# Maxima and sums of eight query blocks in one tile, transposed by one matmul: a kernel of windowed attention mixed with a Fourier layer

## The chip, the cores and the metric

The kernel runs on one core of one Trainium2 chip. The core has five engines that work side by side, each through its own queue in order: TensorE (PE, matrix products; PEld is its weight load), VectorE (DVE), ScalarE (ACT), GpSimd (POOL) and SyncE (SP), which here does nothing but issue DMAs. The metric is the device time of one execution in microseconds (us), lower is better.

## The reference

The input is x of 2048 rows and 512 columns. A gate mixes two layers of it:

```
g = sigmoid((x * gate_w).sum(-1))
a = Cr @ (x @ Wr.T) - Ci @ (x @ Wi.T)      # Fourier layer: 512 wide inside, 2048 x 2048 outside
q, k, v = split(x @ wqkv)                  # 32 heads of 16
p = softmax(q k^T / 4, where 0 <= i - j < 256)
b = (p v) @ wo
out = g * a + (1 - g) * b
```

All values are float32. The inputs make large scores, so the softmax needs its row maxima.

## The kernel before, in words

Dense products (projections, Fourier layer, output) keep float32 precision by a split: every operand is a high part, rounded to the fast matmul type, and a low part, and each product is three fast matmuls (TERMS, line 217).

Attention goes over N = 4 x 32 = 128 steps n: four head groups g of eight heads, 32 blocks of 64 queries. A tile holds four head pairs p (NP = 4), two heads above each other in its 128 rows. Each step does two things, LAG = 20 steps apart.

First, `s_pair(n, p)` (line 314): PE computes the scores of 64 queries of two heads against up to 320 keys (line 324); DVE adds the mask and takes the row minimum of the negated score into a column of `nm` (line 326, one custom instruction and a read of its accumulator, both recorded at that line); ACT takes the exponential and its row sum into a column of `l` (line 329). The scores themselves are then dropped. A group u of eight steps fills 32 columns of `nm` and 32 of `l`: one for each pair and step.

Second, 20 steps later, `t_pair(k, p)` (line 386) computes the transposed scores with the maximum already subtracted, because the maxima stand as extra rows (96 to 99) of `ring[0]`: PE (line 393), exponential by ACT (line 394), masking by POOL (lines 399 and 403). `pv` (line 406) multiplies with the values (line 420) into a PSUM tile `o`; every eighth block the result is multiplied with the reciprocal sums `rl` (line 430), which come from DRAM.

Between the two, the maxima and sums have to turn from columns into rows. That is what the change touches. After group u is complete, in the loop of line 680 at pair p = 2 of a step, behind `pv`:

- `m_rows(u)`: a matmul of `nm` with the identity transposes it into a PSUM tile (line 336); DVE writes minus it as high and low part (lines 339, 340); SP stores that to `m_scr[u]` in DRAM (line 341).
- `l_rows(u)`: DVE takes the reciprocal of `l` (line 350); a second matmul transposes it into another PSUM tile (line 352); DVE copies it to `lt` (line 354); SP stores it to `l_scr[u]` in two pieces (line 357).
- `m_ring(u)`, one step later: ACT's queue loads `m_scr[u]` into rows 96 to 99 of `ring[0]` (line 346).

These two matmuls have full float32 operands, which PE runs as two passes each; a pass has its own weight load.

All DMAs through `ld` (line 55) are issued by SP in order and are recorded at line 56. So one queue holds the stores above, the loads of the ring (`ring<-qk_scr`), of values (`vr<-v_scr`), of Fourier matrices (`raw<-cr`, `raw<-ci`) and of the Fourier layer's inner results (`big<-ab_scr`).

PSUM tiles of scores, transposes and output blocks come from one pool of four buffers (`ps_a`, tag "st"): whoever takes a buffer waits until the last reader of what it held before is done.

What sets the order: on PE it is the program's (line 673). Between the attention's matmuls, `fill` (line 665) takes a fixed number of dense matmuls from the generator `dense`, so PE's queue always holds some. On DVE, ACT, POOL and SP a scheduler, which simulates the kernel while it is built, chooses the order. `make_pad` (line 298) builds, from the ring, the block-diagonal query tiles (`pad`) that the scores of the following steps use as weights. `load_split` and `split_raw` (lines 97 to 105) load a piece of a Fourier matrix into `raw` and split it, by casts at line 80 and subtractions at line 81.

Of the kernel before, what the change touches and what calls it, by code (L numbers as in the profile page):

```python
# [7 lines left out]
F32 = mybir.dt.float32  # L8
# [6 lines left out]
P = 128  # L15
# [4 lines left out]
NP = 4  # L20
# [12 lines left out]
def fnet_window_mix(ctx: ExitStack, tc: tile.TileContext, xT, x, wqk, wv, wr, wi, cr, ci, wo, gw, out):  # L33
    nc = tc.nc
# [3 lines left out]
    st = ctx.enter_context(tc.tile_pool(name="st", bufs=3))  # L38
    ev = ctx.enter_context(tc.tile_pool(name="ev", bufs=5))
    at = ctx.enter_context(tc.tile_pool(name="at", bufs=2))  # L40
    ps_a = ctx.enter_context(tc.tile_pool(name="ps_a", bufs=4, space=PSUM))
# [9 lines left out]
    l_scr = [dram.tile([NP, 2, 512], F32, name=f"l_scr{i}") for i in range(16)]  # L51
# [3 lines left out]
    def ld(dst, src):  # L55
        mark("sp", nc.sync.dma_start(dst, src))

    def f(ap):
        return ap.bitcast(F32)
# [4 lines left out]
    def mark(e, ins):  # L64
        last[e] = ins.ins

    @contextmanager
    def behind(*engines):
        with ExitStack() as es:
            for e in engines:  # L70
                if e in last:
                    es.enter_context(tc.issue_after(last[e]))
            yield
# [51 lines left out]
    with tc.manual_schedule(engines={mybir.EngineType.Activation, mybir.EngineType.DVE, mybir.EngineType.SP}):  # L125
# [12 lines left out]
        for dk in range(DK):  # L138
            c = slice(dk * 256, dk * 256 + 256)
# [17 lines left out]
    ident = const.tile([P, P], F32, name="ident")  # L157
# [6 lines left out]
    for t, edges in ((half, ((0, 16, 32, 48, 64, 80), (16, 32, 48, 64, 80, 96))), (mrow, ((96, 98), (98, 100)))):  # L164
        nc.gpsimd.memset(t, 0.0)
        for h in range(2):
            for i, e in enumerate(edges[h]):
                a = t[:, h:h + 1]
# [3 lines left out]
    def clear_rows(i, ss):  # L172
        nc.gpsimd.memset(f(ring[i][96:128, :, ss * 512:(ss + 1) * 512]), 0.0)
# [7 lines left out]
    def clear_pads():  # L181
        for t in vpad:
            nc.gpsimd.memset(t, 0.0)
        for t in pads[1]:
            nc.gpsimd.memset(f(t[96:128]), 1.0)
            for h in range(2):
                a = t[96:128, :, 64 * h:64 * h + 64]
                nc.vector.tensor_scalar(a, f(a), mrow[96:128, h:h + 1], None, op0=OP.mult)
# [109 lines left out]
    def make_pad(i, n):  # L298
        if not 0 <= n < NG * NB:
            return  # L300
        t = pads[i][n % NPAD]
        b = n % NB
        with behind(*(("act", "dve") if n < NPAD else ())):
            for h in range(2):
                src, dst = f(ring[i][:96, :, b * BQ:(b + 1) * BQ]), t[:96, :, 64 * h:64 * h + 64]
                if i and h:
                    nc.scalar.activation(dst, src, AF.Copy, scale=half[:96, h:h + 1])  # L307
                else:
                    nc.vector.tensor_scalar(dst, src, half[:96, h:h + 1], None, op0=OP.mult)  # L309
        PAD[i, n] = t  # L310

    ML = {}

    def s_pair(n, p):
        j = n % NB
        u, jj = divmod(n, 8)
        if jj == 0 and p == 0:
            ML[u] = [at.tile([P, NP * 8], F32, name="nm"), at.tile([P, NP * 8], F32, name="l")]
        nm, l = ML[u]
        k0 = max(0, (j - 4) * BQ)  # L320
        w = (j + 1) * BQ - k0
        c = slice(p * 8 + jj, p * 8 + jj + 1)
        ps = ps_a.tile([P, 512], F32, name="s", tag="st")
        nc.tensor.matmul(ps[:, :w], PAD[0, n][:, p], ring[1][:, p, k0:k0 + w], start=True, stop=True)  # L324
        sm = at.tile([P, WIN], F32, name="sm", bufs=3)
        mark("dve", nc.vector.tensor_tensor_reduce(out=sm[:, :w], in0=ps[:, :w], in1=mask[:, WIN - w:],  # L326
                                                   scale=1.0, scalar=3e38, op0=OP.add, op1=OP.min,
                                                   accum_out=nm[:, c]))
        mark("act", nc.scalar.activation(sm[:, :w], sm[:, :w], AF.Exp, bias=nm[:, c], scale=-1.0,  # L329
                                         accum_out=l[:, c]))  # L330

    def m_rows(u):
        U = u % 4
        nm = ML[u][0]
        pt = ps_a.tile([P, 512], F32, name="s", tag="st")
        nc.tensor.matmul(pt[:32, :P], nm, ident, start=True, stop=True)
        hl = at.tile([32, 2, 2, 64], F32R, name="mhl", bufs=1)
        m = pt[:32, :P].rearrange("c (a r) -> c a r", a=2)
        nc.vector.tensor_scalar(hl[:, :, 0], m, -1.0, None, op0=OP.mult)
        nc.vector.scalar_tensor_tensor(hl[:, :, 1], m, -1.0, f(hl[:, :, 0]), op0=OP.mult, op1=OP.subtract)  # L340
        ld(m_scr[u].rearrange("x p (j r) -> (p j) x r", r=64), f(hl[:]).rearrange("c a h r -> c (a h) r"))

    def m_ring(u):
        U = u % 4
        with behind("act"):
            nc.scalar.dma_start(f(ring[0][96:100, :, U * 512:(U + 1) * 512]), m_scr[u])

    def l_rows(u):
        l = ML.pop(u)[1]
        nc.vector.reciprocal(l, l)  # L350
        pt = ps_a.tile([P, 512], F32, name="s", tag="st")
        nc.tensor.matmul(pt[:32, :P], l, ident, start=True, stop=True)
        lt = at.tile([32, P], F32, name="lt", bufs=1)
        nc.vector.tensor_copy(lt, pt[:32, :P])
        for a in range(2):
            ls = l_scr[u]
            ld(bass.AP(tensor=ls.tensor, offset=ls.offset + a * 512, ap=[[1024, NP], [64, 8], [1, 64]]),
               lt[:, 64 * a:64 * a + 64])

    OT = {}  # L360
    V2 = {}
# [4 lines left out]
    def v_load(n):  # L366
        if n >= NG * NB:
            return
        g, kb = divmod(n, NB)
        raw = at.tile([P, 4, 64], F32, name="vr", bufs=1)  # L370
        for h in range(2):
            ld(raw[64 * h:64 * h + 64].rearrange("r (c j) x -> r c j x", j=2),
               v_scr[kb // 4][:, :, h, g, :].rearrange("c (j r) x -> r c j x", r=64))
        VR[n] = raw

    def v_spread(n):
        if n >= NG * NB:
            return
        raw = VR.pop(n)
        v2 = vpad[n // 4 % 2]  # L380
        for h in range(2):
            r = slice(64 * h, 64 * h + 64)
            nc.gpsimd.tensor_copy(v2[r, :, :, 16 * h:16 * h + 16], raw[r].rearrange("r j (p d) -> r j p d", d=16))  # L383
        V2[n // 4] = v2
# [262 lines left out]
    def need(key):  # L647
        while key not in have:
            next(stream)
# [3 lines left out]
    def ring_ahead(n):  # L653
        nonlocal loaded
        while loaded < 16:
            g, ss = divmod(loaded, 4)
            if n >= 32 * g + 8 * ss:
                need(("qk", g, ss))
            if ("qk", g, ss) not in have or n - LAG < 32 * (g - 1) + 8 * ss + 9:
                break  # L660
            with behind(*(("sp",) if g == 0 else ())):
                ring_load(g, ss)
            loaded += 1

    def fill(n):
        nonlocal quota
        rate = FILL_FIRST if n < LAG else FILL_SEQ if "proj" in have else FILL_PROJ
        quota += rate / 2
        while quota >= 1:
            next(stream, None)  # L670
            quota -= 1
# [3 lines left out]
    maxima = sent = 0  # L675
# [4 lines left out]
    for n in range(N + LAG + 2):  # L680
        if n in (1, 3, 5):
            for i in range(2):
                clear_rows(1 - i, (n + 1) // 2)
        if n == 7:
            clear_pads()
        k = n - LAG
        ring_ahead(n + 1)
        if -4 <= k < N - 4 and k % 4 == 0:
            for c in range(2):
                need(("v", (k + 4) % NB // 2 + c))  # L690
            with behind(*(("sp",) if k < 4 else ())):
                v_load(k + 4)
        if -4 <= k and k % 4 == 3:
            v_spread(k + 1)
        if n == 0:
            make_pad(0, 0)
        for p in range(NP):
            if n < N:
                s_pair(n, p)
            fill(n)  # L700
            if 0 <= k < N:
                t_pair(k, p)
            if p == 0:
                make_pad(0, n + 1)
                if k >= -1:
                    make_pad(1, k + 1)
            fill(n)
            if p == 2 and sent < maxima:
                m_ring(sent)
                sent += 1  # L710
            if p == 2 and k % 3 == 0:
                for j in range(k - 3, k):
                    if 0 <= j < N:
                        pv(j)
                if maxima < 16 and n > 8 * maxima + 8:
                    m_rows(maxima)
                    l_rows(maxima)
                    maxima += 1
    attention_done()
    for _ in stream:  # L720
# [45 lines left out]
```

## Time and profile before

| | us |
|---|---|
| median of 3 runs | 873.67 |
| lowest and highest | 871.34, 877.32 |
| profiled execution: its own time | 873.98 |
| profiled execution: span of the profile | 872.2 |
| mean granted TensorE clock | 0.998 |

The page of the profile gives the costliest groups of instructions. A line there reads: source line, engine, operation, output and inputs by the program's names, shapes, count, then busy time in us and mean ns of one, then the engine's idle time just before them and what ended it.

```profile
L451 PE MATMUL dc<-big,hi 128*128 128x512 f32 x1024 | 356.0, 396 | 0.0
L329 ACT ACTIVATE sm<-sm,nm 128x320 f32<-128x320 f32 (+4 forms) x512 | 277.9, 544 | 49.4 <-DVE nm L326 47.9
L326 DVE CUSTOM_DVE_ANT_0 sm<-s,mask 128x320 f32<-128x320 f32 (+4 forms) x512 | 231.7, 461 | 95.8 <-PE s L324 75.3
L324 PE MATMUL s<-ring,pad 128*128 128x320 f32 (+4 forms) x512 | 158.4, 309 | 4.3 <-DVE nm L326 3.9
```

Matmuls overlap, so the mean of one is more than what it adds to the queue. The answers about the lines of the change, in ns (minimum, median, maximum), are:

```profile
L336 PE MATMUL s<-ident,nm x32: 272/273/297, 73.2 to 681.0; 128*32 128x128 f32 x32
L352 PE MATMUL s<-ident,l x32: 272/273/273, 73.4 to 681.2; 128*32 128x128 f32 x32
L339 DVE TENSOR_SCALAR mhl<-s x16: 274/279/279, 73.6 to 681.3; 32x128 fp32r<-32x128 f32 x16
L354 DVE COPY lt<-s x16: 268/278/280, 73.8 to 681.5; 32x128 f32<-32x128 f32 x16
L350 DVE RECIPROCAL l<-l x16: 336/343/353, 64.2 to 664.2; 128x32 f32<-128x32 f32 x16
```

Sixteen groups, two passes each, make 32 records for a matmul. Attention with its groups lies between 34 and 753 us of the span; the rest is the start and the end of the dense work.

### The profile page before, as it was taken

Reading aid. Unit: us, or ns where it says so; the run is one execution under the profiler, and the core shown is the slowest. Engines: PE = TensorE matmul, PEld = TensorE weight load, DVE = VectorE, ACT = ScalarE, POOL = GpSimd, SP = SyncE. Lnnn points to the kernel's source line nnn. Section 1 sums busy time; section 2 is a strip of 40 time slices with the busy share of each in tenths; the row PEclk is TensorE's granted clock in tenths of the full one; section 3 lists DMA queues with packets and bytes.
Section 4 is the critical chain, followed back from the end, with each engine's and each line's share of the span. In section 5 each row is a group of like instructions: output and inputs, shape, how many; then the busy total and the mean of one; then the engine's idle time right before and its main releaser. Section 6 shows DMA issues by size and latency. Waiting matters only on the chain.

```text
span 872.2 us, 17214 instructions
## 1 busy us (share of the span) xinstructions
PE 860.1 (99%) x5192; PEld 693.5 (80%) x5192; DVE 601.9 (69%) x1966; ACT 581.4 (67%) x1793; POOL 387.8 (44%) x1067
## 2 busy tenths in 40 slices
PE   9999999999999999999999999999899999999998
PEld 7888778787878778788787887878678787788886
DVE  4588986667879987778787777878585444564431
ACT  5488799888988888788788877878676454111110
POOL 9100154445536746656465666554466665200000
PEclk9999999999999999999999999999999999999999
DMA  7865686465758537634355353589644332376541
GB/s 244 286 218 172 217 253 191 161 207 174 235 171 262 173 95 222 173 116 154 121 148 151 121 143 122 149 282 293 209 144 139 117 119 103 127 265 191 190 145 49
DMA packets 90829, 153.70 MB, mean 176 GB/s; under 512 B 26864, under 2 KB 35824, under 8 KB 90736
## 3 DMA queue, kind: packets, MB, share of 16 engines
q1 hardware_dynamic: 89984, 151.42, 55.3%
q10 hardware_dynamic: 752, 1.18, 0.4%
q8 instruction: 41, 0.67, 0.3%
q14 instruction: 52, 0.43, 0.2%
HBM read 104.60 MB, written 47.97 MB: 175 GB/s over the span
## 4 chain that ended last, share of the span: by engine, by line
PE 91%; DMA 5%; DVE 2%; ACT 1%; issue 0%; SPq 0%; DVEq 0%; ACTq 0%
PE dc L451 39%; PE dab L265 9%; PE s L324 8%; PE o L420 8%; PE dqk L243 8%; PE t L393 8%; PE dv L265 5%; PE t L638 5%; DMA qk_scr<-hl 2%; DMA ring<-qk_scr 1%; DMA big<-ab_scr 1%; DVE sm L326 1%; DMA pt<-wqk 1%; PE s L231 0%; DVE pad L309 0%
## 5 line engine op out<-in xcount | busy, mean ns | idle before, releaser
L451 PE MATMUL dc<-big,hi 128*128 128x512 f32 x1024 | 356.0, 396 | 0.0
L399 POOL TENSOR_SCALAR_AFFINE_SELECT pt<-pt 64x128 f32<-64x128 f32 x512 | 192.7, 376 | 274.0 <-ACT pt L394 257.7
L329 ACT ACTIVATE sm<-sm,nm 128x320 f32<-128x320 f32 (+4 forms) x512 | 277.9, 544 | 49.4 <-DVE nm L326 47.9
L326 DVE CUSTOM_DVE_ANT_0 sm<-s,mask 128x320 f32<-128x320 f32 (+4 forms) x512 | 231.7, 461 | 95.8 <-PE s L324 75.3
L394 ACT ACTIVATE pt<-t 128x320 f32<-128x320 f32 (+4 forms) x512 | 209.0, 412 | 93.0 <-PE t L393 91.1
L451 PEld LDWEIGHTS dc<-big,hi 128*128 128x128 f32 x1024 | 186.6, 188 | 32.8 <-issue 2.5
L451 PE MATMUL dc<-big,lo 128*128 128x512 f32 x512 | 201.8, 394 | 0.0
L403 POOL TENSOR_SCALAR_AFFINE_SELECT pt<-pt 64x128 f32<-64x128 f32 x448 | 165.6, 370 | 0.0
L324 PE MATMUL s<-ring,pad 128*128 128x320 f32 (+4 forms) x512 | 158.4, 309 | 4.3 <-DVE nm L326 3.9
L393 PE MATMUL t<-ring,pad 128*128 128x320 f32 (+4 forms) x512 | 154.7, 302 | 0.3 <-DVE nm L326 0.3
L309 DVE TENSOR_SCALAR pad<-ring,half 96x256 fp32r<-96x256 f32 x384 | 120.4, 356 | 28.0 <-PE t L393 22.5
L324 PEld LDWEIGHTS s<-ring,pad 128*128 128x128 f32 x512 | 96.1, 188 | 38.6 <-issue 8.5
L393 PEld LDWEIGHTS t<-ring,pad 128*128 128x128 f32 x512 | 96.3, 188 | 18.7 <-DVE nm L326 1.4
L451 PEld LDWEIGHTS dc<-big,lo 128*128 128x128 f32 x512 | 96.4, 188 | 10.8
L81 DVE TENSOR_TENSOR lo<-raw,hi 128x512 fp32r<-128x512 f32 x146 | 98.9, 708 | 1.3 <-PE dc L451 1.3
L329 ACT ACTIVATION_READ_ACCUMULATOR sm<-sm,nm 128x1 f32 x512 | 99.1, 194 | 0.0
L265 PE MATMUL dab<-hi,big 128*128 128x512 f32 x256 | 91.1, 396 | 0.9 <-DVE hl L88 0.9
L243 PE MATMUL dqk<-big,hi 128*128 128x512 f32 x240 | 86.6, 394 | 1.1 <-DVE hl L86 0.5
L80 DVE CAST hi<-raw 128x512 fp32r<-128x512 f32 x142 | 59.0, 456 | 37.8 <-PE dc L451 36.3
L420 PE MATMUL o<-pt,vpad 128*32 128x320 f32 (+4 forms) x1408 | 74.4, 353 | 0.0
L383 POOL COPY vpad<-vr 64x256 f32<-64x256 f32 x64 | 26.0, 407 | 91.3 <-DMA vr<-v_scr 71.6
L307 ACT ACTIVATE pad<-ring,half 96x256 fp32r<-96x256 f32 x128 | 64.2, 502 | 0.0
(83 smaller groups left out, 777.3 us busy)
## 6 DMA issues: line engine op xcount, KB each, us to landing
qk_scr<-hl SPq DMA_DIRECT2D x32, 512.0 KB
ring<-qk_scr SPq DMA_DIRECT2D x32, 512.0 KB
raw<-cr SPq DMA_DIRECT2D x32, 512.0 KB
raw<-ci SPq DMA_DIRECT2D x32, 512.0 KB
ab_scr<-hl SPq DMA_DIRECT2D x20, 512.0 KB
big<-ab_scr SPq DMA_DIRECT2D x20, 512.0 KB
ring<-qk_scr SPq DMA_DIRECT2D x32, 256.0 KB
r_scr<-ev SPq DMA_DIRECT2D x28, 256.0 KB
```

The lines of the kernel that those rows point to most:

```text
L243: nc.tensor.matmul(ps, w[a][:, c:c + 128], XT[dk, ss][:, b], start=n == 0, stop=n == 11)
L265: nc.tensor.matmul(ps, XT[dk, ss][:, a, c * 128:(c + 1) * 128], wh[b], start=n == 0, stop=n == 11)
L309: nc.vector.tensor_scalar(dst, src, half[:96, h:h + 1], None, op0=OP.mult)
L324: nc.tensor.matmul(ps[:, :w], PAD[0, n][:, p], ring[1][:, p, k0:k0 + w], start=True, stop=True)
L326: mark("dve", nc.vector.tensor_tensor_reduce(out=sm[:, :w], in0=ps[:, :w], in1=mask[:, WIN - w:], scale=1.0, scalar=3e38, op0=OP.add, op1= ...
L329: mark("act", nc.scalar.activation(sm[:, :w], sm[:, :w], AF.Exp, bias=nm[:, c], scale=-1.0, accum_out=l[:, c]))
L393: nc.tensor.matmul(ps[:, :w], PAD[1, n][:, p], ring[0][:, p, q0:q0 + w], start=True, stop=True)
L394: nc.scalar.activation(pt[:, p, :w], ps[:, :w], AF.Exp, scale=-1.0)
L399: nc.gpsimd.affine_select(a, a, pattern=[[0, 2], [1, 64]], compare_op=OP.is_ge, fill=0.0, base=0, channel_multiplier=-1)
L403: nc.gpsimd.affine_select(a, a, pattern=[[0, 2], [-1, 64]], compare_op=OP.is_gt, fill=0.0, base=0, channel_multiplier=1)
L420: nc.tensor.matmul(OT[g, sb][32 * p:32 * p + 32, q - sb * 512:e - sb * 512], v2[:, p], pt[:, p, q - q0:e - q0], start=first, stop=kb == 8 ...
L451: nc.tensor.matmul(ps, w[a][:, s8 * 128:(s8 + 1) * 128], ab[SC[i]][:, b], start=i == 0 and a + b == 0, stop=i == 15 and a == 1)
```

## The change

The maxima and the sums of a group become the two halves of one tile `ml`, whose 64 columns one matmul with the identity transposes. Maxima are then rows 0 to 31 of the result and reciprocal sums rows 32 to 63, so the copy reads and writes partitions 32 to 63. `m_rows` and `l_rows` become one function, `ml_rows`, in which the reciprocal comes before the matmul and the copy after the two instructions on the maxima.

```diff
-            ML[u] = [at.tile([P, NP * 8], F32, name="nm"), at.tile([P, NP * 8], F32, name="l")]
-        nm, l = ML[u]
+            ML[u] = at.tile([P, 2, NP * 8], F32, name="ml")
+        nm, l = ML[u][:, 0], ML[u][:, 1]
...
-    def m_rows(u):
-        U = u % 4
-        nm = ML[u][0]
+    def ml_rows(u):
+        ml = ML.pop(u)
+        nc.vector.reciprocal(ml[:, 1], ml[:, 1])
         pt = ps_a.tile([P, 512], F32, name="s", tag="st")
-        nc.tensor.matmul(pt[:32, :P], nm, ident, start=True, stop=True)
+        nc.tensor.matmul(pt[:64, :P], ml.rearrange("p x c -> p (x c)"), ident, start=True, stop=True)
         hl = at.tile([32, 2, 2, 64], F32R, name="mhl", bufs=1)
         m = pt[:32, :P].rearrange("c (a r) -> c a r", a=2)
         nc.vector.tensor_scalar(hl[:, :, 0], m, -1.0, None, op0=OP.mult)
         nc.vector.scalar_tensor_tensor(hl[:, :, 1], m, -1.0, f(hl[:, :, 0]), op0=OP.mult, op1=OP.subtract)
         ld(m_scr[u].rearrange("x p (j r) -> (p j) x r", r=64), f(hl[:]).rearrange("c a h r -> c (a h) r"))
+        lt = at.tile([64, P], F32, name="lt", bufs=1)
+        nc.vector.tensor_copy(lt[32:64], pt[32:64, :P])
+        for a in range(2):
+            ls = l_scr[u]
+            ld(bass.AP(tensor=ls.tensor, offset=ls.offset + a * 512, ap=[[1024, NP], [64, 8], [1, 64]]),
+               lt[32:64, 64 * a:64 * a + 64])
...
-    def l_rows(u):
-        l = ML.pop(u)[1]
-        nc.vector.reciprocal(l, l)
-        pt = ps_a.tile([P, 512], F32, name="s", tag="st")
-        nc.tensor.matmul(pt[:32, :P], l, ident, start=True, stop=True)
-        lt = at.tile([32, P], F32, name="lt", bufs=1)
-        nc.vector.tensor_copy(lt, pt[:32, :P])
...
-                    m_rows(maxima)
-                    l_rows(maxima)
+                    ml_rows(maxima)
                     maxima += 1
```

More of the change, by code (lines that the diff above doesn't have):

```diff
@@ L346, in m_ring @@
             nc.scalar.dma_start(f(ring[0][96:100, :, U * 512:(U + 1) * 512]), m_scr[u])
-    def l_rows(u):
-        l = ML.pop(u)[1]
-        nc.vector.reciprocal(l, l)
-        pt = ps_a.tile([P, 512], F32, name="s", tag="st")
-        nc.tensor.matmul(pt[:32, :P], l, ident, start=True, stop=True)
-        lt = at.tile([32, P], F32, name="lt", bufs=1)
-        nc.vector.tensor_copy(lt, pt[:32, :P])
[L355 to L358, printed above, removed]
     OT = {}
```

## The prediction

> **What bounds the kernel now.** I read the page first: shares of engines, then the chain of work that ended last.
>
> ```profile
> span 872.2 us, 17214 instructions
> PE 860.1 (99%) x5192; PEld 693.5 (80%) x5192; DVE 601.9 (69%) x1966; ACT 581.4 (67%) x1793; POOL 387.8 (44%) x1067
> PE 91%; DMA 5%; DVE 2%; ACT 1%; issue 0%; SPq 0%; DVEq 0%; ACTq 0%
> ```
>
> TensorE (PE) is busy or waiting on itself nearly throughout, at the full granted clock (9s in every slice, 0.998 mean). So what an edit saves on PE's queue counts, unless a wait behind it takes it back; what it saves or adds on VectorE (DVE, 69%) or on SP's queue counts only where PE stands still for it. So I read two more views: PE in order of time around one group's transposes, and the places where PE does stand still.
>
> The timeline of PE at group 2 of 16 (columns: start us, duration us, engine, line, operation):
>
> ```profile
> 138.80 0.73 PE L420 MATMUL o<-pt,vpad 128*32 128x192 f32 x16
> 139.35 0.38 PE L336 MATMUL s<-ident,nm 128*32 128x128 f32 x2
> 139.56 0.38 PE L352 MATMUL s<-ident,l 128*32 128x128 f32 x2
> 139.88 0.41 PE L324 MATMUL s<-ring,pad 128*128 128x320 f32 x1
> ...
> 142.79 0.31 PE L393 MATMUL t<-ring,pad 128*128 128x320 f32 x1
> ```
>
> A transpose is recorded as two passes (x2). Durations overlap, so I count from start to start: the second transpose starts 0.21 to 0.22 us after the first; the trace's nanosecond starts give 109 ns from pass to pass in all groups, 203 ns from the last pass to the next score matmul (147 ns is usual between a 320-wide matmul and its follower), and 251 ns behind that score matmul instead of 147. The last two belong to the switch back from the 32-column form, and are paid as often by one transpose as by two.
>
> PE's longest stops, from its timeline, and the chain of waits in the second place (columns: start, duration, what; in brackets the idle time before it):
>
> ```profile
> 95.98 0.41 PE L324 MATMUL s<-ring,pad 128*128 128x320 f32 x1 [1.05 <-DVE nm L326]
> 616.17 0.45 PE L324 MATMUL s<-ring,pad 128*128 128x320 f32 x1 [2.84 <-DVE nm L326]
> 614.84 0.87 DVE L309 TENSOR_SCALAR pad<-ring,half 96x256 fp32r<-96x256 f32 x3 [3.65 <-DMA ring<-qk_scr]
> 591.97 9.32 DMA big<-ab_scr
> 601.90 12.84 DMA ring<-qk_scr
> ```
>
> The first is group 1, right behind its two transposes. The second is the one large stop of the run: DVE can't build the next query pads (line 309) until the last ring load lands, 12.84 us after its issue at 601.90, behind a pile of 512 KB loads in SP's queue; behind DVE the scores wait, and PE with them.
>
> **The PE part.** One matmul of two passes goes from each of 16 groups; 64 columns of weights instead of 32 are loaded for the pass that stays, and as many columns (128) stream through. The row that is nearest says the pass is paced by streaming: in the o matmuls of 32-column weights and the same 128 moving columns (line 420), four passes to four column quarters take 110 ns together, though each has its own 110 ns weight load; and those with 192 moving columns take 164. So I take 109 ns for each pass that is left: 2 x 109 = 0.218 us saved in a group. The other bound is a pass paced by its weight load: 110 ns for 32 columns and 188 for 128 give 136 for 64 on a straight line, 188 at worst. That makes the saving 4 x 109 - 2 x 136 = 0.164 us, and 0.060 at worst.
>
> The Trainium skill (TensorE: Matmul & The Clock Gate, section "LDWEIGHTS (loading the stationary operand)") has load time follow the columns, columns / 1.2 ns; that speaks against the wider tile, with 27 ns more a load. The rows agree in the slope (78 ns for 96 columns), not in the constant; by that rule, with nothing hidden, the saving is an estimated 0.164 us a group, the middle of the bounds above.
>
> In group 1 I count nothing. DVE is busy with hardly a gap from 94.83 to 115.6 there, and has as much to do as before. PE's next score (95.98) would find its PSUM buffer one score earlier, because one buffer less is taken, and the next would start 0.7 us earlier; but PE that runs ahead of a full DVE waits for it later. Bounds: 0 to -0.9 us. So: 15 x 0.218 = 3.27 us saved, 0.9 to 3.5 by the bounds.
>
> **The DVE part.** As many instructions of the same shapes: reciprocal 0.34 us, L339 0.28, L340 0.27, copy 0.28, four a group in both kernels. The built program of the changed kernel has them in another order: before it is L339, copy, a score's pair, L340; after it is L339, a score's pair, two pads (0.26 each), L340, copy. In groups 12 and 14 one more instruction lies ahead. In group 2, L339 ends at 140.04 as now, the score's pair starts near 140.11, and the copy ends near 140.11 + 0.42 + 2 x 0.26 + 0.21 + 0.28 = 141.54. Who waits for it: the one PSUM buffer of the transpose is free only then. The built program gives that buffer to the score (t) matmul that now starts at 142.79, so 142.57 after: 1.0 us to spare (0.4 in group 12, where the copy ends near 557.8). I price it at 0, by that cover. That the one matmul waits for the reciprocal costs nothing: it ran 9 us ahead in group 0 (64.2 against 73.2).
>
> The pads that DVE now does ahead of L340 are for a block 5 us on; nobody waits.
>
> **SP and ACT.** Three small stores a group, in a new order: rows of maxima, then sums, sums. L340 ends 0.3 us later (141.3; 0.9 in group 12), so m_scr does, and the ACT queue waits for its landing before it loads the ring's rows (line 346). Now that load is issued 3.3 us behind the store in most groups, 2.43 in group 0, and 1.68 in group 15, so 1.68 us is enough for a landing: no wait follows (in group 0 perhaps 0.1 us of ACT, unseen by PE). SP's issues move past those stores by 0.6 us each; nothing in the chain stands on them, with one exception.
>
> **The exception, 600 to 620 us.** The scheduler, seeing other times, has issued one load in another place: `raw<-ci` (512 KB, now at 600.28) comes after the ring load and two more transfers (512 + 256 KB), and DVE's split of it (two casts 0.76 us, two subtractions 0.60 each, now done at 608.41 to 610.8) comes after the ring's pads and two scores. Two things follow. The ring load has 512 KB less ahead: from the rows of issues, a 512 KB load of that stretch gets through in about 1.3 us, so pads start near 613.5 and PE's stop shortens by up to 1.3. Then DVE reaches the split near 613.5 + 0.79 + 0.82 = 615.1 and waits for raw. The same bytes as now are through at 614.84; then 768 KB more, at the 209 to 282 GB/s of the page's slices there 2.7 to 3.7 us: 617.8. With the split, 1.96, DVE is at 619.8 where it now is at 616.45: 3.3 us late. How much of it reaches PE no row tells; PE has few PSUM buffers to run ahead, but DVE has 15% to spare afterwards (34.1 of the 40 us from 620 to 660 busy). Bounds -1.3 and +3.3; I take +1.5, above the middle because the wait stands in DVE's order of instructions.
>
> What was saved before 600 us is not lost in this stop: the loads ahead of the ring (`big<-ab_scr`) each wait for a PE matmul that frees their tile, so the pile begins earlier as well.
>
> **Sum.** The profiled execution took 873.98 us (span 872.2 and 1.8 around it): -3.27 + 1.5 = -1.8, so 872.2. Against the median of the three runs, 873.67, that is 871.9. These runs lie between 871.34 and 877.32.
>
> **Rivals.**
> - *All of it arrives.* The ring lands earlier, raw in time, group 1 gives its 0.7: 873.67 - 3.5 - 1.3 - 0.7 = 868.2. For it: PE is the chain for 91%. Against it: raw's place. Chance 0.22.
> - *Slower: DVE stands before raw.* If raw takes from its issue (about 603.8) the 12.84 us that the ring load took, and the 768 KB ahead of it are in addition (3 us), it lands at 619.7, and DVE is 5.2 us late instead of 3.3; if all of that reaches PE: 873.67 - 3.27 + 5.2 = 875.6. It decides from a landing later than 617.7 on; from there each us is one us. For it: the queue's 12.84. Against it: 8.1 us is all that raw had between issue and use now. Chance 0.25.
> - *The passes are paced by the loads.* 15 x 0.060 saved, with +1.5: 874.3. No saving worth the name: the change doesn't do what it says. Against it: the 110 ns for four o passes. Chance 0.10.
> - *The late copy holds the buffer.* If DVE is over 1.0 us later than in my sum at every group, the t matmul waits: from there on 14 groups lose each us more; 0.8 us a group is 873.67 - 3.27 + 11.2 = 881.6. Against it: the spare time above. Chance 0.05.
>
> The forecast itself, between 870 and 873.5: 0.38.
>
> **Range and chances.** 868.2 to 875.6 holds the forecast and three rivals; with the scatter of a median (runs lie 3.6 us above and 2.3 below theirs) I set 867.4 to 876.6, and leave out the late copy and some of the edges, 2 in 10. 1% of 873.67, about what a measurement of this kernel can tell from no change, is 8.7 us: below 864.9 lies no case that I can name (0.05, for more waits shortened than I see); above 882.4 the late copy's upper part and a longer stop before raw (0.08). Within: 0.87.
>
> **What would show it.** PE transposes at line 336: 32 records instead of 64, about 109 ns apart, groups 0.2 us shorter from the last o matmul to the next score (over 136 ns apart: paced by loads). In PE's waits no line with `lt`. Near 95.98 no idle time behind the transpose. Near 613 to 620, DVE's wait before the pads below 3.65 us, and a new one before the cast of raw; PE's stops there in sum 4.3 us against 2.84 (below 2: the first rival; over 6: the second). ACT with no longer wait before line 346's load. What would make it wrong: a difference of more than 5 us, or any new PE wait that repeats in all 16 groups.

## The result, and the profile after

The changed kernel takes 876.97 us (median of 19 runs, 875.76 to 882.87); the kernel before, beside it on the same chip, 873.62 (19 runs, 871.02 to 877.32). The ratio is 1.0049, with a 95% interval of 1.0037 to 1.006. So the change makes the kernel slower by about half a per cent, where the sum said 1.8 us faster, and the median lies 0.4 us above the range. The profiled execution of the changed kernel took 875.87 us, 1.9 more than the one before.

The page of the changed kernel, its span, engines and shares of the chain:

```profile
span 873.9 us, 17118 instructions
PE 860.5 (98%) x5160; PEld 688.0 (79%) x5160; DVE 604.4 (69%) x1966; ACT 580.0 (66%) x1793; POOL 386.2 (44%) x1067
PE 85%; DMA 7%; DVE 5%; issue 1%; ACT 1%; ACTq 0%; SPq 0%; DVEq 0%
```

32 instructions fewer on PE, as many as were removed, and no less time busy. PE's share of the chain (the work that ended last, followed back) is down from 91% to 85%, the DMAs' up from 5% to 7% and DVE's from 2% to 5%: something that is not PE has come into the path.

Where it sits can be read exactly, because PE's order of instructions is the same in both kernels but for the transposes. I matched the other 5,128 matmuls of the two traces one by one and took how much later each starts after the change. The lag changes in few places (us, stretches by the time of the kernel before):

```
stretch           lag changes by   what lies there
0 to 185               -0.11       groups 0 to 2: -1.3 at group 1, given back by 106
185 to 196             +1.22       behind group 3
310 to 322             +1.54       behind group 6
436 to 446             +1.62       behind group 9
558 to 572             +1.20       behind group 12
600 to 626             -3.47       the large stop of before, and what follows
the other groups       -0.02 to -0.10 each
640 to 646             +0.50       behind group 14
at the end             +1.67
```

Four losses of 1.2 to 1.6 us, 5.58 together, each right behind one of the groups 3, 6, 9 and 12; one gain of 3.47 at the place of the old stop; and hardly anything from the removed passes. I take these in turn.

**The four losses.** The chain of waits of the changed kernel behind group 3 (start, duration, what):

```profile
187.68 4.32 DMA m_scr<-mhl
...
192.02 0.64 ACTq L352
...
193.36 0.33 ACT pt L388
...
193.74 0.41 PE s L324
```

The store of the maxima, issued at 187.68, takes until 192.0; ACT's queue then issues the load of the ring's rows (line 352 now, 346 before), does the exponentials queued behind it, and only then PE has a free buffer for the next score. Before, this load was issued 3.3 us behind the store (186.48 to 189.76), and ACT did not wait for it. After, the distances are 4.34, 4.87, 4.94 and 4.72 us in groups 3, 6, 9 and 12, and 1.57 to 3.8 in the others. The waits name it too (total us, times, longest): a line that the kernel before does not have, and one that was 2.8 us in 6 waits before.

```profile
ACT sm L329 <- DMA m_scr<-mhl: 3.5, 2, 2.1
PEld s L324 <- ACT pt L388: 8.4, 13, 1.7
```

Why these four groups? SP's queue has the answer. In group 6, first before and then after the change (start, duration, instruction; `x2` is two DMAs):

```profile
309.25 0.65 SPq L56 DMA_DIRECT2D l_scr<-lt  x1
310.01 0.38 SPq L56 DMA_DIRECT2D m_scr<-mhl  x1
310.44 0.63 SPq L56 DMA_DIRECT2D l_scr<-lt  x1
311.12 1.22 SPq L56 DMA_DIRECT2D ring<-qk_scr  x2
```

```profile
310.64 1.19 SPq L56 DMA_DIRECT2D ring<-qk_scr  x2
311.92 0.54 SPq L56 DMA_DIRECT2D m_scr<-mhl  x1
312.51 1.33 SPq L56 DMA_DIRECT2D l_scr<-lt  x2
```

The two ring loads, 512 and 256 KB, are now ahead of the 32 KB of maxima. The scheduler has put them there in exactly the groups 3, 6, 9 and 12. By the DMA queue's bytes the store is through 1.0 to 1.1 us after its issue before, and 3.3 to 3.9 after. The Trainium skill (DMA: Bandwidth & Descriptors, section "Queues, rings and completion order") says that the descriptors of one ring are consumed in order on each DMA engine; these rows agree: the small store gets its turn when the large loads ahead of it have had most of theirs (in group 6 its first bytes move 3.0 us after its issue, where the loads' bytes are nearly through).

**The transposes.** The changed kernel's matmul and its weight load (busy us, mean ns), and its PE timeline at group 2:

```profile
L336 PE MATMUL s<-ident,ml 128*64 128x128 f32 x32 | 6.9, 298 | 0.0
L336 PEld LDWEIGHTS s<-ident,ml 128*64 128x64 f32 x32 | 3.1, 134 | 3.9 <-issue 3.5 <-DVE hi L80 0.2
```

```profile
139.47 0.43 PE L336 MATMUL s<-ident,ml 128*64 128x128 f32 x2
139.84 0.41 PE L324 MATMUL s<-ring,pad 128*128 128x320 f32 x1
```

From the first pass to the score 0.37 us, where two transposes took 0.53 (139.35 to 139.88). But the first pass starts later: by the starts in ns, 203 ns after the last `o` matmul instead of 89. The second pass follows 160 ns after the first, not 109. In ns, from the last `o` matmul to the score: before 89 + 109 + 109 + 109 + 203 = 619, after 203 + 160 + 202 = 565. That saves 54 ns in a group, not 218. The weight loads at group 2, before and then after, show where the late start sits:

```profile
139.24 0.22 PEld L336 LDWEIGHTS s<-ident,nm 128*32 128x32 f32 x2
```

```profile
139.47 0.19 PEld L336 LDWEIGHTS s<-ident,ml 128*64 128x64 f32 x2 [0.20 <-issue]
```

By the starts in ns, the first load of 32 columns starts 108 ns ahead of its pass, while `o` matmuls still go out; the one of 64 columns starts only 2 ns ahead of its pass, and its second load 53 ns behind the first pass, where with 32 columns it is 2 ns. What holds the wider loads back is not shown here. In groups 0 and 1, where the matmul ahead is not one of 32 columns, the first pass starts 319 ns after it in both kernels, and 0.19 us is saved.

**The old large stop**, near 616 us, is shorter (DVE's pads and their wait, PE's score, and the cast of raw):

```profile
617.69 0.88 DVE L309 TENSOR_SCALAR pad<-ring,half 96x256 fp32r<-96x256 f32 x3 [2.29 <-DMA ring<-qk_scr]
...
619.02 0.41 PE L324 MATMUL s<-ring,pad 128*128 128x320 f32 x1 [0.98 <-DVE ml L326]
...
620.63 0.87 DVE L80 CAST hi<-raw 128x512 fp32r<-128x512 f32 x2 [1.25 <-DMA raw<-ci]
```

DVE waits 2.29 us for the ring instead of 3.65, PE 0.98 instead of 2.84. PE comes there 4.7 us later than before, the ring only 2.85 later (617.69 against 614.84).

The shorter stop is 1.86 of the 3.47 us. The rest is PE's clock: behind the stop of before the granted clock fell to a half, behind the shorter one it did not. Windows of the kernel before, then of the changed one (stretch; us, busy time and number of instructions of PE, PEld, DVE, ACT and POOL; then the granted clock, the DMA share and GB/s):

```profile
616.00:618.00 2.00, 1.82 (x6) 1.51 (x6) 1.03 (x6) 1.84 (x6) 0.69 (x3) 0.60 1.02 392
618.00:620.00 2.00, 2.00 (x18) 0.61 (x20) 0.00 (x0) 0.55 (x3) 0.39 (x2) 0.54 1.11 329
```

```profile
618.00:620.00 2.00, 1.02 (x6) 0.89 (x6) 1.38 (x7) 0.99 (x4) 0.00 (x0) 1.00 1.03 406
620.00:622.00 2.00, 2.00 (x27) 0.76 (x25) 1.37 (x3) 0.85 (x3) 1.48 (x4) 1.00 1.04 394
```

From the score behind the stop to the next score, over the same matmuls, PE took 4.73 us before (616.17 to 620.90) and 3.18 after (619.02 to 622.20).

### The profile page after: what moved, and what is told of

The parts are those of the page before. It is cut to its first block, busy times and chain, and to the rows that moved or that the text cites. A ratio compares the mean times of both kernels' runs of the same rounds, so it can differ in the third digit from the quotient of the medians.

```text
span 873.9 us, 17118 instructions
## 1 busy us (share of the span) xinstructions
PE 860.5 (98%) x5160; PEld 688.0 (79%) x5160; DVE 604.4 (69%) x1966; ACT 580.0 (66%) x1793; POOL 386.2 (44%) x1067
## 4 chain that ended last, share of the span: by engine, by line
PE 85%; DMA 7%; DVE 5%; issue 1%; ACT 1%; ACTq 0%; SPq 0%; DVEq 0%
PE dc L445 37%; PE dab L265 8%; PE o L414 8%; PE s L324 8%; PE t L387 7%; PE dqk L243 7%; PE dv L265 5%; PE t L632 5%; DMA ring<-qk_scr 2%; DMA m_scr<-mhl 2%; DMA qk_scr<-hl 2%; DVE sm L326 1%; DVE pad L309 1%; DVE lo L81 1%; DMA big<-ab_scr 1%
## 5 line engine op out<-in xcount | busy, mean ns | idle before, releaser
L329 ACT ACTIVATE sm<-sm,ml 128x320 f32<-128x320 f32 (+4 forms) x512 | 277.1, 542 | 53.1 <-DVE ml L326 47.2
L329 ACT ACTIVATION_READ_ACCUMULATOR sm<-sm,ml 128x1 f32 x512 | 98.9, 193 | 0.0
```

## The experiments

Two theories stood at first. Theory 1: the loss is ACT's queue standing for the landing of a store that SP issues behind ring loads. Theory 2: the transpose itself, wider and one buffer for both halves, makes PE and DVE slower, and the long store is a by-product. In all of them "the four stops" are those behind groups 3, 6, 9 and 12; their sum is the change of lag in the four stretches above, against the kernel named.

**1. Ring loads behind the stores** (changed kernel; the other end of the pair in SP's queue; the first line stands at the end of `ml_rows`):

```diff
+        last["rows"] = last["sp"]
...
-            with behind(*(("sp",) if g == 0 else ())):
+            with behind(*(("sp",) if g == 0 else ("rows",))):
                 ring_load(g, ss)
```

> The changed kernel, but every ring load from group 1 of heads on is issued by SP behind the three small stores of the last transposed group. Theory 1 (in groups 3, 6, 9 and 12 SP issues 768 KB of ring loads ahead of the 32 KB store of maxima, which then lands 4.3 to 5 us after its issue; ACT's queue stands before the load that reads it, and PE stops 0.67 + 0.99 + 1.43 + 0.94 = 4.0 us): the landings come back to under 2.5 us, the four stops go, about 4 us less than the changed kernel: 873.0 against 877.0, ratio to before 0.998 to 1.001. Theory 2 (the loss is in the wider transpose itself: 160 ns a pass, and the PSUM buffer held by the later copy): unchanged, ratio 1.004 to 1.006.

875.59 us, ratio 1.0028 (1.0007 to 1.0048). The four stops are gone (-5.47 us against the changed kernel), and in these groups the row load is issued 2.8 to 2.9 us behind the store. But 1.88 us, against the changed kernel, came back between 262 and 300 us, where DVE now stood 1.97 us for a load of x, and 2.3 us between 600 and 626. So theory 1 gets the place right and the time wrong (expected 0.998 to 1.001): the cure costs elsewhere.

**2. The same wait put into the kernel before:** its two separate transposes stay, and the store of the maxima is issued behind the ring loads in groups 3, 6, 9 and 12. The main lines are below; in these groups the store also moves to the start of the next step, behind the ring loads:

```diff
...
+        with behind(*(("ring",) if u in (3, 6, 9, 12) else ())):
+            ld(m_scr[u].rearrange("x p (j r) -> (p j) x r", r=64), f(hl[:]).rearrange("c a h r -> c (a h) r"))
...
+            last["ring"] = last["sp"]
```

> The kernel before with its two transposes, but in groups 3, 6, 9 and 12 the store of maxima is issued behind the two ring loads, as the changed kernel has it. Theory 1: four stops of PE of 0.7 to 1.4 us each behind ACT's wait, 4 us more than before: 877.6, ratio 1.0035 to 1.006. Theory 2: no wider transpose, so no loss: ratio 0.999 to 1.001.

879.52 us, ratio 1.0068 (1.0047 to 1.0089). The stops appear in the kernel before, in the same four groups, with 4.6 to 5.45 us from store to row load and 7.54 us of lag, more than expected. 3.64 of them lie behind group 9: there the stop, 1.78 us at 444.11, was followed by a granted clock of 0.64 and 0.51 in the windows 444 to 446 and 446 to 448 us. SP in group 6:

```profile
311.61 1.21 SPq L56 DMA_DIRECT2D ring<-qk_scr  x2
312.91 0.53 SPq L56 DMA_DIRECT2D m_scr<-mhl  x1
```

No 64-column transpose is in this kernel. The wait alone makes the loss.

**3. The row load a step later** (changed kernel, SP's order as it is; ACT meets the late store later):

```diff
-    maxima = sent = 0
+    maxima = sent = at_n = 0
...
-            if p == 2 and sent < maxima:
+            if p == 2 and sent < maxima and n > at_n:
                 m_ring(sent)
...
                     ml_rows(maxima)
                     maxima += 1
+                    at_n = n + 1
```

> The changed kernel, but ACT loads the rows of maxima into the ring one step (about 5 us) later; SP's order as in the changed kernel. Theory 1: the store still lands 4.3 to 5 us after its issue in the four groups, but ACT's queue no longer meets it, and the four stops go: 873.0, ratio 0.998 to 1.001. Theory 2: unchanged, 1.004 to 1.006.

872.85 us, ratio 0.9996 (0.9981 to 1.0011). In the four groups the load is issued 6.5 to 6.9 us behind the store, and the four stops are gone (-5.54 us against the changed kernel), though SP's order is the changed kernel's. New: 2.8 us lost between 106 and 139 us, at a stop of 1.88 us at 121.94 with a granted clock of 0.69 and 0.50 in the two windows of 2 us behind it.

**4. Two quarters:** one tile and one PSUM buffer, but two matmuls of 32 columns, into rows 0 to 31 and 32 to 63.

```diff
-        nc.tensor.matmul(pt[:64, :P], ml.rearrange("p x c -> p (x c)"), ident, start=True, stop=True)
+        for x in range(2):
+            nc.tensor.matmul(pt[32 * x:32 * x + 32, :P], ml[:, x], ident, start=True, stop=True)
```

> The changed kernel's one tile and one PSUM buffer, but transposed by two matmuls of 32 columns into rows 0 to 31 and 32 to 63. Theory 2: four passes of 32 columns in two column quarters run two by two, 2 x 110 ns for both instead of 2 x 160, 0.1 to 0.2 us less in each of 16 groups, and the loss goes: ratio 1.000 to 1.002. Theory 1: the passes are that much shorter, 1.6 to 3.2 us, but the four stops stay: 874 to 875.5, ratio 1.001 to 1.003, with ACT's waits before the load of maxima unchanged. Apart from that it measures the pass.

876.54 us, ratio 1.0041 (1.0026 to 1.0057). The passes of the two halves start 6 to 8 ns apart and run side by side; from the last `o` matmul to the score it is 89 + 6 + 103 + 7 + 202 = 407 ns at group 2, 158 less than with 64 columns. The four stops stay and grow, to 7.1 us, so the time is above what either theory expected. Theory 2 is out: a much cheaper transpose leaves the loss where it was.

**5. Experiments 3 and 4 together.**

> The changed kernel with two edits together: the ring rows loaded a step later (m_ring), and the tile transposed by two 32-column matmuls into rows 0 to 31 and 32 to 63 of one buffer instead of one 64-column matmul. The store of the maxima stays behind the ring loads. Theory 1 (ACT's queue stands for that store's landing): the four stops of PE near 193, 318, 442 and 568 us stay away although the store lands late, and the shorter transposes come on top: below the rows-later run by the 0.15 to 0.3 us a group that the two halves side by side save, 2.4 to 4.8 us, if no other stop grows: 868 to 871, ratio 0.994 to 0.998. Theory 2 (the order of work around the transposes costs, whatever ACT waits for): four stops stay, ratio 1.003 or more.

870.58 us, ratio 0.9979 (0.996 to 0.9998). The four stops stay away. A new one of 1.30 us stands at 597.6, where in group 13 the later row load itself makes ACT wait.

**6. The later load in the kernel before**, as a control: the edit of experiment 3 and nothing else.

> The kernel before, with the ring rows loaded a step later and nothing else. A control for the rows-later run: if the later load is by itself a gain, not only a cure of the new wait, this kernel is faster than before by some us (ratio 0.995). Theory 1: before had no wait of ACT for that landing in these groups (3.3 us from store to load, the store done after 1.1), so there is nothing to gain: ratio 1.000 within 0.0015; and where the load comes too near to its readers in group 1 (a stop near 122 us in the rows-later run) it loses up to 2 us: ratio up to 1.002.

872.96 us, ratio 0.9994 (0.9979 to 1.0009). Nothing to gain, as theory 1 has it: the later load cures a wait that this kernel does not have.

**7. The later load in groups 3, 6, 9 and 12 only**, with the two quarters (in place of experiment 3's line for `at_n`):

```diff
...
                     maxima += 1
+                    at_n = n + (1 if maxima in (4, 7, 10, 13) else 0)
```

> The changed kernel with two 32-column matmuls, and the ring rows a step later in groups 3, 6, 9 and 12 alone, the four in which the store of the maxima stands behind ring loads. Theory 1: the four stops stay away as with the later load in all groups, and the stop that the later load brought in group 1 (2.0 us near 122) goes: 1 to 2 us below the run with it in all groups. If the four stops come back or another one appears, the late load in the other groups did something that theory 1 does not hold.

869.72 us, ratio 0.9958 (0.9943 to 0.9974): faster than both kernels. 0.9 us below experiment 5 by the medians, 1.8 by the ratios. The stop that went is the one at 597.6; the one near 121 us, which I had named, was 0.70 in experiment 5 and is 0.91 here. It is 0.88 in the kernel before, so the later load does not make it.

**8. One line moved:** the copy of the sums written between the two instructions on the maxima, the 64-column matmul kept.

```diff
         nc.vector.tensor_scalar(hl[:, :, 0], m, -1.0, None, op0=OP.mult)
+        lt = at.tile([64, P], F32, name="lt", bufs=1)
+        nc.vector.tensor_copy(lt[32:64], pt[32:64, :P])
         nc.vector.scalar_tensor_tensor(hl[:, :, 1], m, -1.0, f(hl[:, :, 0]), op0=OP.mult, op1=OP.subtract)
...
-        lt = at.tile([64, P], F32, name="lt", bufs=1)
-        nc.vector.tensor_copy(lt[32:64], pt[32:64, :P])
```

> The changed kernel with one matmul of 64 columns, but the copy of the sums written between the two instructions on the maxima, as the kernel before has it on VectorE. By that the built order of SP's queue has the store of the maxima ahead of the ring loads again in groups 3, 6 and 9, and between them in group 12. Theory 1: the stops near 193, 318 and 442 go, the one near 568 goes or halves; store to row load is 3.3 us again; ratio 0.998 to 1.001. Theory 2 (the 64-column pass itself costs): the matmul is the same, so the time stays at that of the changed kernel, ratio 1.004 or more. The passes stay 160 ns apart in either case.

876.11 us, ratio 1.0025 (1.001 to 1.004): the four stops behave as expected, the time does not. SP's queue in groups 6 and 12:

```profile
310.85 0.39 SPq L56 DMA_DIRECT2D m_scr<-mhl  x1
311.29 1.21 SPq L56 DMA_DIRECT2D ring<-qk_scr  x2
```

```profile
557.40 0.56 SPq L56 DMA_DIRECT2D ring<-qk_scr  x1
558.05 0.54 SPq L56 DMA_DIRECT2D m_scr<-mhl  x1
558.64 0.59 SPq L56 DMA_DIRECT2D ring<-qk_scr  x1
```

With the store ahead again, the lag against the kernel before does not move in groups 3, 6 and 9 (+0.03, +0.03, +0.04 us); in group 12, with one ring load still ahead, it grows by 1.75. So the place of one copy on DVE decides SP's order, and SP's order the stops. The rest of the profiled run's loss (+3.8 us at the end) lies elsewhere: +2.0 us from 600 to 626, where the changed kernel has -3.5, and +0.5 behind group 14, as there. Windows of this run there, in the columns as above:

```profile
616.00:618.00 2.00, 0.00 (x0) 0.00 (x0) 0.84 (x4) 0.00 (x0) 0.00 (x0) 0.80 1.03 397
618.00:620.00 2.00, 1.51 (x4) 1.32 (x5) 1.35 (x7) 1.53 (x6) 0.42 (x2) 0.50 1.01 382
620.00:622.00 2.00, 2.00 (x11) 0.78 (x14) 0.00 (x0) 0.86 (x3) 0.65 (x3) 0.50 0.94 241
```

PE stands for 3.76 us, and then works at half the clock until 624: this stop is paid twice.

**9. The changed kernel without its wait:** one matmul of 64 columns, the later load in the four groups. **11. The kernel of experiment 7 again**, on the same chip.

> The changed kernel with its one matmul of 64 columns, and the ring rows a step later in groups 3, 6, 9 and 12 alone: the changed kernel without its new wait and otherwise as it is. Theory 1: the four stops stay away, 4.0 us in sum, so ratio 0.9995 to 1.001 (1.0049 less 0.0046); above the same kernel with two matmuls of 32 columns by what the transposes differ between their trace rows, 8.93 against 6.68 us over 16 groups, 2.25 us: ratio 0.0026 higher than that kernel in the same call. If the wait were a by-product, the ratio stays at 1.003 or more.

> The fastest kernel so far once more (two matmuls of 32 columns, ring rows a step later in groups 3, 6, 9 and 12), on the same chip as the one with a single matmul: ratio 0.994 to 0.998 again, and 0.0026 below the kernel with one matmul of 64 columns. If it comes out at 0.999 or more, the gain found before was the chip's.

Experiment 9: 871.93 us, ratio 0.9995 (0.998 to 1.0011). Experiment 11: 869.39 us, ratio 0.9971 (0.9956 to 0.9986). Without the wait the changed kernel is as fast as the one before, so the wait is worth 1.0049 - 0.9995 (each ratio against the kernel before, run beside it), 0.0054 or 4.7 us; and what is left of the change is worth nothing that this can tell. The two quarters are worth 0.0024, 2.1 us (expected 0.0026).

**10. What sets the 160 ns:** the same 64 columns of weights, loaded for two matmuls that each stream 64 columns instead of 128.

```diff
-        nc.tensor.matmul(pt[:64, :P], ml.rearrange("p x c -> p (x c)"), ident, start=True, stop=True)
+        for a in range(2):
+            nc.tensor.matmul(pt[:64, 64 * a:64 * a + 64], ml.rearrange("p x c -> p (x c)"),
+                             ident[:, 64 * a:64 * a + 64], start=True, stop=True)
```

> The changed kernel with its transpose cut in two along the other axis: the same 64 columns of weights, loaded for each of two matmuls that stream 64 columns of the identity instead of 128. It asks what sets the 160 ns from pass to pass. If a pass is its load and its streaming one behind the other, half the streaming (109 ns for 128 columns in the o matmuls, 55 for 64) leaves 105 to 110 ns; if it is paced by the load alone, it stays between 134 and 160 ns; if the load is hidden and only streaming counts, 55 to 80 ns. The time is that of the changed kernel within 4 us.

878.14 us, one run. The four passes start 107, 58 and 58 ns apart, in every group, with a load of 132 to 138 ns (132 to 136 in the changed kernel). So the load's recorded time does not pace the passes: 58 is less than half of it. The first gap shrinks from 160 by the 53 ns that are no longer streamed, but it keeps some 50 ns more than the gaps behind it. That extra belongs to the second pass behind the change from one tile width to another: in the kernel before, groups 0 and 1, the same gap is 133 ns where the next ones are 109 (32 columns). In the trace the second weight load starts 54 ns behind the first pass, the later ones 3 ns behind theirs; what delays it is not shown here.

## Why the prediction was wrong

**The step that failed is in the part on SP and ACT:** "so 1.68 us is enough for a landing: no wait follows", and behind it "nothing in the chain stands on them". The 1.68 us were read in group 15, where no ring load stands ahead of the store. In groups 3, 6, 9 and 12 of the changed kernel 768 KB of ring loads do, and the store needed 4.3 to 4.9 us until the row load behind it could go. I listed the new order of the three stores among themselves, and not what the built order had moved ahead of all three. I also stopped at ACT: its wait was priced by itself (0.1 us), and not by the exponentials queued behind it, for which PE's score waits. Experiment 2 makes the loss in the kernel before, by this order alone; experiments 3 and 9 remove it with the order left as it is; experiment 8 removes it in three groups by restoring the order. The sum of the four, 5.6 us in the trace, is more than either of the two terms that I had added up (-3.27 and +1.5).

**The PE part was mis-sized: 0.218 us a group, measured 0.054** (0.19 in groups 0 and 1), about 1.1 us in all instead of 3.27. That lies within my 0.9 to 3.5, but by luck: both bounds were wrong in kind. The nearest row that I took, 109 or 110 ns, holds within a run of passes of one tile width (not "in all groups": behind 128 columns, in groups 0 and 1, the first was 133); the single matmul that is left always comes behind a change of width, and has the exposed first gap (203 ns instead of 89, as its load no longer starts early) and second gap (160 instead of 109). My bound for a pass paced by its load gave the right load (134 measured, 136 by the straight line) and the wrong conclusion, as experiment 10 shows. My test for "paced by the loads" in the list of what would show it, passes over 136 ns apart, was met at 160, without that cause.

By the Trainium skill's rule for the load (TensorE: Matmul & The Clock Gate, section "LDWEIGHTS (loading the stationary operand)"), 32 more columns take an estimated 27 ns more; the trace agrees with 110 to 134. What the rule could not say is how much of a load is seen.

**The DVE part was right in the main.** No PE wait names `lt`, the buffer was free in time, and the lag moves by 0.1 us at most in the groups without ring loads ahead. The exception is group 14, with 0.5: it comes in every kernel with the one tile and in neither of the two built from the kernel before (experiments 2 and 6), so it belongs to the change; its cause is not shown. And what DVE's new order did cost, it cost through SP's queue, as experiment 8 shows.

**Group 1** was counted at nothing, with bounds of 0 to -0.9, since PE that runs ahead of a full DVE waits for it later. So it was: the stop at 95.98 is gone (-1.3 us), and longer stops near 103 and 105 us have taken its place; by 121 us the lag is +0.01.

**The exception, 600 to 620 us,** was right in mechanism and wrong in sign. A ring that is late by less than PE is, a shorter wait before the pads, a new wait before raw's cast (1.25 us): all three are there. But DVE stood 1.25 us for raw, not the 2.7 from 615.1 to 617.8, and PE's stops were 0.98 us and a short one at 643 instead of 4.3: the case of my first rival, at this place. And the sum had no term for the clock: I read a full one throughout, but behind the old stop it was 0.60 and 0.54, and 1.6 of the 3.47 us gained come from that. One sentence of mine fell with it: "what was saved before 600 us is not lost in this stop". In experiment 9 PE reaches 600 us 4.3 us earlier than in the changed kernel and the ring lands only 2.15 earlier (615.54), so half of what was saved there is waited for again, and the longer stop (3.14 us) costs clock besides: at 626 us, in that execution, all 4.3 are gone. The medians say that this is not the rule (0.9995 against 1.0049). The kernel of experiments 7 and 11 shows the scatter: the ring landed at 610.26 in one execution and at 612.36 in the other, with stops of 0.74 and 2.41 us. What decides the landing from run to run is open.

**None of the rivals had the cause.** The one nearest to the measured median, DVE standing before raw with 875.6, had the wrong place. That the median lies only 0.4 us outside the range is luck: in the traces an unforeseen loss of 5.6 us meets a place where +1.5 was forecast and -3.5 came.

## What to carry to other kernels

When an edit lets a scheduler reorder a shared DMA queue, read for every small transfer what stands ahead of it, not only that it is still issued about when it was; a few microseconds of large loads ahead of it are its landing time. If an in-order engine's own queue issues the DMA that depends on it, everything behind that DMA waits, here the exponentials and with them TensorE. And price an instruction that stays by the row of its own neighbourhood: a lone transpose between matmuls of another tile width costs other gaps than one in a row of its kind; here two matmuls of 32 columns in different column quarters were cheaper than one of 64. And price a stop of TensorE with the clock behind it, not by its length alone.

## What the runs showed of the hardware

- Two 32-column matmuls into different quarters of PSUM's partitions start 6 to 8 ns apart and run side by side; the pair costs 158 ns less than one matmul of 64 columns over the same data (407 against 565 ns at group 2). In the Trainium skill (TensorE: Matmul & The Clock Gate, section "The mechanism") weight loads overlap a running matmul only where the row groups differ, though it also names loads into a background weight buffer; here all 128 rows are used by both, the columns differ, and the 7 ns leave no room for a load of 110 ns between them. Which way these loads take, the trace does not show.
- A stop of PE can halve its granted clock, and its length alone does not decide that. Stops of 1.75 us (experiment 1, at 616.6), 1.78 (experiment 2, at 444.1), 1.88 (experiment 3, at 121.9), 2.41 (experiment 11), 2.84 (the kernel before), 3.14 (experiment 9) and 3.76 (experiment 8) were followed by a clock of 0.50. Those of 0.74 (experiment 7), 0.98 (the changed kernel) and 1.66 (experiment 8, at 121.1) were not, but neither were 1.88 (experiment 6, at 601.5) and 2.15 (experiment 2, at 623.1). Summed over the windows, the half clock lasted about 3.4 us each time, and 6.8 behind the two longest stops. In experiment 9 the way from the score behind the stop to the next one took 5.79 us (616.88 to 622.67), where the changed kernel took 3.18. The Trainium skill (TensorE: Matmul & The Clock Gate, section "What's actually happening") gives one idle window of about 3.4 us for this; here 1.75 us were enough. The windows of experiment 11, in the columns as above:

```profile
612.00:614.00 2.00, 0.30 (x1) 0.30 (x2) 1.64 (x7) 0.32 (x1) 0.00 (x0) 0.94 1.03 411
614.00:616.00 2.00, 2.00 (x6) 1.35 (x5) 0.84 (x4) 1.64 (x6) 1.17 (x4) 0.50 1.03 395
```

- The spread of the runs goes with that clock. Of the 23 runs of the kernel before beside experiment 9, the 13 with a mean clock of 1.000 have a median of 871.3 us, the eight with 0.998 one of 873.7; half a clock for 3.4 of 872 us is 0.002.
